# Retention and a mixture of adapters: 64-token steps instead of 128-token chunks, and queries loaded from a second queue

## The chip, the cores and the metric

One core of one Trainium2 chip runs the whole kernel. The metric is the device time of one execution in microseconds. Before the change three runs gave 181.16, 181.38 and 181.57 us, a median of 181.38.

## The reference, cut to what matters

```python
# q, k, v: (8, 8, 576, 64) float32: batch, head, token, feature
scores = scale * np.matmul(q, k.transpose(0, 1, 3, 2))
gamma = 1.0 - 2.0 ** (-5.0 - np.arange(H))
rel = pos[:, None] - pos[None, :]
Dmat = np.where(rel >= 0, gamma[:, None, None] ** rel[None], 0.0)
ret = scores * Dmat                      # causal decay instead of a softmax
x = (ret @ v)                            # then (4608, 512): heads side by side

logits = x @ w_gate                      # 8 experts
topk = the two largest logits of a token, w = their softmax
out = x + sum over both of  w * (x @ A[e]) @ B[e]     # A: 512 x 16, B: 16 x 512
```

As the decay is a power of the distance, the sum over all earlier tokens can be carried as a state: k (scaled) times v, 64 x 64 for each head. A token then needs the scores inside its own piece of the sequence and one product of its query with the state.

## The kernel before, in words

**Units.** A unit is a piece of the sequence for two of the eight batches, b = 0 and 1, with all eight heads. The sequence of 576 tokens has four chunks of 128 tokens (c = 0 to 3) and a rest of 64 (c = 4). Each full chunk gives four units, one for each pair of batches; the rest gives two units that hold four batches each, as two pieces of 64 tokens. That is NU = 18 units: 0 to 3 are chunk 0, 4 to 7 chunk 1, up to 16 and 17, the rest.

**Stages of a unit on TensorE**, by the names that the text uses, with their lines:
- T (L272): transposes k and q of a unit, heads in pairs, in halves of 64 tokens.
- S (L390) and SL (L369): scores. Each full unit has "early" tokens (the first 64) and "late" ones. S takes early keys against all 128 queries, SL late keys against late queries. VectorE multiplies S (L404, L408, L412) by a mask, or by the decay in chunk 0, and writes it next to the transposed queries, in the tile xq; SL gets its own mask (L422).
- U (L442): the unit's addition to the state, k times v over all 128 tokens. VectorE adds it to the old state (L461), and the sum is half of the next chunk's tile blk.
- X (L500; L481 in chunk 0) and XL (L523): the output. A tile blk holds, for each batch, 64 rows of state and 64 rows of early v; with the scores and the queries facing them, one product over 128 rows gives the state's part and the early part together. XL adds the late v times the late scores.
- Z (L571): logits and adapters' inner products, x times AW (136 columns).
- P (L552), B (L644), Y (L663): P transposes the weighted inner products, B transposes x back to tokens by rows, in two banks by odd and even head, and Y adds the adapters' second product into the same banks.

**The engines beside it.** ScalarE (ACT) takes most results out of PSUM: kT and xq after T (L296), xT after X (L541), zs after Z (L584), zT after P (L560), osb after Y (L680), and it copies the queries to the other 64 partitions (shift_q, L324). It also makes the sigmoid of the routing (L609). VectorE (DVE) masks, adds the state and finds the two largest logits (L594 to L599). GpSimd (POOL) scales k and q by the powers of gamma (L171), makes the routing's weights cm and zc (L619, L621), and copies v into place (place_v, L345 to L347: the early rows into blk, and one late half into vl).

**Rounds.** The body of the loop at L870 is a round t, from 3 to 17, in which unit t has its scores, unit p = t - 1 its output X and Z, unit z = t - 2 its P, B, Y, and unit t + 1 is transposed. The order of the calls is the order of the instructions on each engine. Loads of unit t + 3 and stores of unit t - 3 are all issued on SyncE's queue (SP), one after another, in a list of jobs: load_jobs, store_jobs. on_pe (L119) sums an estimate of TensorE's time, and each job is tied to the matmul at which it falls due (LOAD_NS after the last load, STORE_NS after the last store). A load of 256 KB is one of q, k, v of one batch of a unit, in runs of 64 float32. Matmuls on float32 are two records each in the trace, transposes one.

**After the rounds** the outputs of the last units are finished with their own order of calls (L906 to L948).

## Time and profile before

| | before |
|---|---|
| median of three runs | 181.38 us |
| profiled execution | 182.06 us |
| its span, first to last instruction | 180.3 us |
| granted TensorE clock, mean | 0.997 |
| busy: TensorE, weight loads, VectorE, ScalarE, GpSimd | 94%, 84%, 51%, 63%, 65% of the span |
| data moved | 39.01 MB, of which 29.11 MB are read from HBM and 9.44 MB written |
| chain that ended last | TensorE 63%, SyncE's queue 15%, DMA 9%, GpSimd 5% |

How to read it: the span lies inside the time of the execution, 1.8 us less. TensorE's row counts matmuls from start to modelled end, and they overlap, so a stage's cost is best read from the start of its first matmul to the start of the next stage's. A row of a timeline has the start and the duration of a merged run of instructions in us, engine, line, operation, what is written from what, shape (stationary rows*columns, then the moving tile) and the count; what stands in brackets is idle time of the engine before it and what ended it. In a row of windows stand the stretch, its length, the busy time of PE, PEld, DVE, ACT and POOL with the number of instructions, the granted clock, the mean share of the DMA engines' time, and GB/s. A share over 1 comes from packets that overlap on an engine.

### The profile page before, as it was taken

Reading aid. Unit: us, or ns where it says so; the run is one execution under the profiler, and the core shown is the slowest. Engines: PE = TensorE matmul, PEld = TensorE weight load, DVE = VectorE, ACT = ScalarE, POOL = GpSimd, SP = SyncE. Lnnn points to the kernel's source line nnn. Section 1 sums busy time; section 2 is a strip of 40 time slices with the busy share of each in tenths; the row PEclk is TensorE's granted clock in tenths of the full one; section 3 lists DMA queues with packets and bytes.
Section 4 is the critical chain, followed back from the end, with each engine's and each line's share of the span. In section 5 each row is a group of like instructions: output and inputs, shape, how many; then the busy total and the mean of one; then the engine's idle time right before and its main releaser. Section 6 shows DMA issues by size and latency. Waiting matters only on the chain.

```text
span 180.3 us, 9353 instructions
## 1 busy us (share of the span) xinstructions
PE 168.9 (94%) x4135; PEld 151.8 (84%) x4135; DVE 92.8 (51%) x171; ACT 114.3 (63%) x217; POOL 116.5 (65%) x176
## 2 busy tenths in 40 slices
PE   7989999989998999999999999999999999899960
PEld 2677888879887999899999999989999999899940
DVE  0082666554656383929282819190919191715540
ACT  3524296558584767676767575757777777875460
POOL 0453675699978668686969695949495958762000
PEclk9999999999999999999999999999999999999998
DMA  6999999999998998999999998989999887803306
GB/s 142 250 249 214 255 224 235 247 249 229 258 240 203 227 231 225 252 231 232 237 224 253 257 256 195 250 215 246 235 240 255 216 220 200 284 5 122 120 0 233
DMA packets 119216, 39.01 MB, mean 216 GB/s; under 512 B 114180, under 2 KB 114564, under 8 KB 119176
## 3 DMA queue, kind: packets, MB, share of 16 engines
q1 hardware_dynamic: 118304, 37.82, 84.6%
q8 instruction: 32, 0.52, 1.2%
q10 hardware_dynamic: 728, 0.47, 0.9%
q0 software_dynamic: 144, 0.13, 0.4%
q14 instruction: 8, 0.07, 0.1%
HBM read 29.11 MB, written 9.44 MB: 214 GB/s over the span
## 4 chain that ended last, share of the span: by engine, by line
PE 63%; SPq 15%; DMA 9%; POOL 5%; issue 3%; DVE 1%; ACT 1%; POOLq 0%; ACTq 0%
PE pz L571 15%; PE px L500 12%; SPq L164 11%; PE a L442 7%; DMA q<-in_q_dram 6%; PE ps_s L390 5%; PE po L644 4%; PE pt_k L272 4%; DMA v<-in_v_dram 3%; PE a L369 3%; PE pt_q L272 3%; PE po L663 3%; PE px L523 3%; SPq L160 2%; PE pzt L552 2%
## 5 line engine op out<-in xcount | busy, mean ns | idle before, releaser
L171 POOL TENSOR_TENSOR k<-k,pack 128x512 f32<-128x512 f32 x35 | 35.9, 1043 | 11.9 <-PE pt_k L272 10.4
L541 ACT COPY xT<-px 128x512 f32<-128x512 f32 x35 | 20.2, 590 | 27.5 <-PE px L500 20.4
L571 PE MATMUL pz<-AW,xT 128*128 128x136 f32 x288 | 37.6, 283 | 0.0
L571 PEld LDWEIGHTS pz<-AW,xT 128*128 128x128 f32 x288 | 34.7, 190 | 0.2
L594 DVE MAX8 m<-zs 128x8 f32<-128x8 f32 x32 | 3.8, 161 | 55.9 <-ACT zs L584 55.9
L408 DVE TENSOR_TENSOR xq<-ps_s,pack 64x1024 f32<-64x1024 f32 x24 | 29.3, 1220 | 1.7 <-PE ps_s L390 1.3
L171 POOL TENSOR_TENSOR q<-q,pack 128x512 f32<-128x512 f32 x28 | 28.8, 1042 | 1.9 <-DMA q<-in_q_dram 1.9
L500 PE MATMUL px<-xq,blk 128*64 128x128 f32 (+1 forms) x480 | 27.3, 264 | 0.1
L500 PEld LDWEIGHTS px<-xq,blk 128*64 128x64 f32 x480 | 24.2, 137 | 0.7 <-issue 0.5
L347 POOL COPY blk<-v 64x512 f32<-64x512 f32 x32 | 19.5, 608 | 1.3
L442 PE MATMUL a<-v,k 128*64 128x64 f32 x512 | 19.1, 225 | 1.0 <-issue 0.8
L390 PE MATMUL ps_s<-xq,kT 64*64 64x128 f32 (+1 forms) x640 | 19.3, 260 | 0.0
L442 PEld LDWEIGHTS a<-v,k 128*64 128x64 f32 x512 | 16.6, 138 | 2.8 <-issue 1.5
L619 POOL TENSOR_TENSOR cm<-ge,sg 128x16 f32<-128x16 f32 x16 | 3.5, 221 | 22.8 <-DVE xq L408 17.4
L680 ACT COPY osb<-po 128x512 f32<-128x512 f32 x34 | 18.0, 581 | 0.0
L461 DVE TENSOR_TENSOR blk<-a,blk 64x512 f32<-64x512 f32 x24 | 16.4, 685 | 0.2
L390 PEld LDWEIGHTS ps_s<-xq,kT 64*64 64x64 f32 x640 | 16.0, 134 | 0.5 <-issue 0.4
L296 ACT COPY xq<-pt_q 128x1024 f32<-128x1024 f32 x16 | 16.3, 1019 | 0.3 <-PE pt_q L272 0.3
L324 ACT COPY xq<-xq 64x512 f32<-64x512 f32 x26 | 16.1, 617 | 0.6
L296 ACT COPY kT<-pt_k 128x1024 f32<-128x1024 f32 x15 | 15.2, 1014 | 1.2 <-PE pt_k L272 0.6
L272 PEld LDWEIGHTS pt_k<-pack,k 64*128 64x128 f32 x288 | 10.9, 139 | 5.5 <-issue 3.7
L272 PE MATMUL pt_k<-pack,k 64*128 64x64 f32 x288 | 13.5, 230 | 1.5 <-POOL zc L621 0.8
(68 smaller groups left out, 261.2 us busy)
## 6 DMA issues: line engine op xcount, KB each, us to landing
out_dram<-osb SPq DMA_DIRECT2D x35, 256.0 KB, 4.2
q<-in_q_dram SPq DMA_DIRECT2D x28, 256.0 KB, 4.9
k<-in_k_dram SPq DMA_DIRECT2D x26, 256.0 KB, 4.9
v<-in_v_dram SPq DMA_DIRECT2D x24, 256.0 KB, 4.7
v<-in_v_dram SPq DMA_DIRECT2D x6, 512.0 KB, 6.3
k<-in_k_dram SPq DMA_DIRECT2D x5, 512.0 KB, 6.3
q<-in_q_dram SPq DMA_DIRECT2D x4, 512.0 KB, 6.4
A_nat<-in_moe_A_dram SPq DMA_DIRECT2D x1, 256.0 KB
```

Source lines behind the costliest of these rows:

```text
L164: nc.sync.dma_start(out=nt(u, w), in_=rows(w, 2 * bp, 2, 128 * c, 128))
L171: engines[b].tensor_tensor(out=tl[:, b * H : b * H + H, :], in0=tl[:, b * H : b * H + H, :], in1=g[:, c, :].unsqueeze(2).broadcast_to((128 ...
L272: nc.tensor.matmul(ps[r][:, b, hp, :], lhsT=src[hf(r), b * H + 2 * hp : b * H + 2 * hp + 2, :], rhs=id64[hf(r), :], is_transpose=True, sta ...
L296: nc.scalar.copy(out=tl.rearrange("p b a t j -> p t (b a) j"), in_=st[u]["p2" + w].rearrange("p r b a j -> p r (b a) j"),)
L347: engs[b].tensor_copy(out=blk(u)[hf(b), b], in_=vn[0:64, b * H : b * H + H, :])
L390: nc.tensor.matmul(ps[hf(b), int(ho == b), hp, qc], lhsT=kT[hf(ho), b, hp, kc], rhs=qT[hf(ho), b, hp, qc], start=(hp == 0 and qc.start == ...
L408: nc.vector.tensor_tensor(out=dst, in0=src, in1=m, op=ALU.mult)
L442: nc.tensor.matmul(a[hf(1 - b), ho, 1, hp, :], lhsT=kn[:, h, :], rhs=vn[:, h, :], start=(hp == 0), stop=True, skip_group_check=True,),
L500: nc.tensor.matmul(px[b][hf(ho), hp, qc], lhsT=bk[:, b, 2 * hp + ho, :], rhs=facing(u, b, ho)[:, hp, qc], start=(hp == 0 and t == 0 and no ...
L541: nc.scalar.copy(out=dst, in_=src)
L571: nc.tensor.matmul(st[u]["pzb"][b] if "pzb" in st[u] else pz[:, b, :], lhsT=st[u]["xT"][b][:, dt, :], rhs=AW[:, dt, :], start=(dt == 0), s ...
L680: copy(out=s["osb"][:, :, :, ho, :], in_=s["po"][ho])
```

## The change

From chunk 1 on, a unit goes by two steps of 64 tokens, as the rest did already:
- S computes the scores inside each 64-token step for both batches; SL, its mask and XL are left to chunk 0. mask_e takes one step (i) of both batches at a time.
- U gives two sums, one a step, in products over 64 tokens. add_state(t, 0) makes the state that the second step starts from, add_state(t, 1) that of the next chunk.
- A unit has two tiles, step(u, 0) and step(u, 1), each with a state half and a v half. v is loaded straight into them, in two loads of 64 partitions; place_v is left to chunk 0.
- X takes each step's 64 queries against that step's tile.
- shift_q copies the queries of a step to the other partitions, for both batches, on GpSimd.
- B transposes 128 x 128 with a whole identity (ident, a float32 copy of ident16 made by GpSimd), one bank for each batch; Y adds in three pieces of 192, 192 and 128 columns; one copy on ScalarE takes both batches out.
- A round is put in another order: X of p, U of t, S of t, P, B, Y of z, Z of p, then both transposes of t + 1. TensorE's stream has 513 instructions in such a round.
- From round 5 on, that is for units 8 to 17, q is loaded from ScalarE's queue, after evict_z; k, v and the stores stay on SyncE's, with LOAD_NS 1000 for 1150 and STORE_NS 650 for 745.
- The end has another order, and the last unit's outputs are taken out in quarters by VectorE and ScalarE.

```diff
-    LOAD_NS, STORE_NS = 1150, 745
+    LOAD_NS, STORE_NS = 1000, 650
...
+    def shift_q(u):
+        for s in range(2):
+            nc.gpsimd.tensor_copy(
+                out=of_step(st[u]["x2"][hf(1 - s)], s), in_=of_step(st[u]["qT"][hf(s)], s)
+            )
...
+        ps = st[u]["ps"] = pp.tile([128, 2, 2, HP, 64], FP32, tag="s", name="ps_s")
+        for b in range(2):
+            for hp in range(HP):
+                for s in range(2):
+                    for ho in range(2):
+                        on_pe(
+                            31,
+                            nc.tensor.matmul(
+                                ps[hf(s), int(ho == s), b, hp, :],
+                                lhsT=kT[hf(ho), b, hp, hf(s)],
+                                rhs=qT[hf(ho), b, hp, hf(s)],
...
+        a = st[u]["a"] = [
+            pp.tile([128, H, Dh], FP32, tag=f"o{s}", name=f"a{s}") for s in range(2)
+        ]
+        for h in range(H):
+            for s in range(2):
                 for b in range(2):
...
+    def add_state(u, s):
+        dst, o = next_state(u) if s else (step(u, 1), hf(0))
+        for b in range(2):
+            nc.vector.tensor_tensor(
+                out=dst[o, b], in0=st[u]["a"][s][hf(b)], in1=step(u, s)[hf(1 - s), b], op=ALU.add
+            )
...
                             nc.tensor.matmul(
-                                px[b][hf(ho), hp, qc],
-                                lhsT=bk[:, b, 2 * hp + ho, :],
-                                rhs=facing(u, b, ho)[:, hp, qc],
+                                px[b][hf(ho), hp, hf(s)],
+                                lhsT=step(u, s)[:, b, 2 * hp + ho, :],
+                                rhs=facing(u, s, ho)[:, b, hp, hf(s)],
...
+                    nc.tensor.matmul(
+                        st[u]["po"][b][:, dt, :],
+                        lhsT=st[u]["xT"][b][:, dt, :],
+                        rhs=ident,
+                        is_transpose=True,
...
+        for b in bs:
+            for ms in (slice(0, 192), slice(192, 384), slice(384, 512)):
...
     for t in range(3, NU):
...
-        jobs += lk + lq[:1] + out_jobs[:1] + lq[1:] + out_jobs[1:] + lv
+        if t < 5:
+            jobs += lk + lq[:1] + out_jobs[:1] + lq[1:] + out_jobs[1:] + lv
+        else:
+            jobs += lk + out_jobs + lv
         routing_3(z)
         routing_4(z)
-        scores(t)
-        if nxt < NU:
-            place_v(nxt, pool2)
         if t + 2 < NU:
             scale_(t + 2, "k", pool2)
             scale_(t + 2, "q", pool2)
-        if is_full(p):
+        if units[p][0] == 0:
             stage_XL(p)
+        stage_X(p)
+        evict_x(p)
         if is_full(t):
             stage_U(t)
-            add_state(t)
-        stage_X(p)
-        evict_x(p)
+        if units[t][0] == 0:
+            stage_SL(t)
+        elif is_full(t):
+            add_state(t, 0)
+        stage_S(t)
...
+        for i in range(2):
+            mask_e(t, i)
+        if units[t][0] > 0 and is_full(t):
+            add_state(t, 1)
+        if not is_full(t):
+            stage_B(z, "a", (0,))
+        stage_P(z)
+        evict_z(z)
+        for b in range(2 if 5 <= t < NU - 3 else 0):
+            load_half(t + 3, "q", b, nc.scalar)
+        stage_B(z, "a", (0, 1) if is_full(t) else (1,))
+        stage_Y(z)
+        evict_o(z)
         if nxt == NU:
             break
-        stage_T(nxt, "k")
-        evict_T(nxt, "k")
-        stage_B(z)
-        stage_T(nxt, "q")
-        stage_P(z)
-        evict_z(z)
-        evict_T(nxt, "q")
         stage_Z(p)
         routing_1(p)
-        shift_q(nxt, (nc.scalar,) * 2 if t + 2 < NU else pool2)
-        stage_Y(z)
-        evict_o(z)
+        stage_T(nxt, "k", "a")
+        evict_T(nxt, "k")
+        stage_T(nxt, "q", "s")
+        evict_T(nxt, "q")
         routing_2(p)
+        if units[nxt][0] > 0:
+            shift_q(nxt)
...
+    for b in range(2):
+        end_route_1(y, b)
+    stage_B(y, "a")
+    for b in range(2):
+        end_route_2(y, b)
+    for b in range(2):
+        stage_X(u, (b,), ("x1", "s"))
+        evict_x(u, (b,))
+    stage_P(y, tag="x0")
+    evict_z(y)
...
+    stage_Y(y)
+    evict_o(y)
+    end_bank(u, "s")
+    stage_Z(u, (1,))
...
+    stage_Y(u)
+    for b in range(2):
+        evict_end(u, b)
```

More of the change, by code (lines that the diff above doesn't have):

```diff
@@ L556, in stage_P, with evict_z @@
             )
[L558 to L561 removed]
+    def evict_z(u, bs=(0, 1)):
+        if "zT" not in st[u]:
+            st[u]["zT"] = mo.tile([128, 2, 128], FP16, tag="zT", name="zT")
+        b = slice(bs[0], bs[-1] + 1)
+        nc.scalar.copy(out=st[u]["zT"][:, b], in_=st[u]["pzt"][:, b])
     def stage_Z(u, bs=(0, 1)):
@@ L671, in stage_Y, with evict_o @@
                 )
-    def evict_o(u, vector=False):
+    def evict_o(u):
         s = st[u]
-        s["osb"] = mo.tile(
-            [128, 2, HP, 2, 64], FP32, tag="osb", name="osb", bufs=3, align_bytes=256
-        )
-        for ho in range(2):
-            copy = nc.vector.tensor_copy if vector and not ho else nc.scalar.copy
-            copy(out=s["osb"][:, :, :, ho, :], in_=s["po"][ho])
+        s["osb"] = mo.tile([128, 2, Dm], FP32, tag="osb", name="osb", bufs=3, align_bytes=256)
+        nc.scalar.copy(out=s["osb"], in_=s["po2"].rearrange("p b a m -> p b (a m)"))
     def end_route_1(u, b):
@@ L848 @@
     stage_U(2)
-    add_state(2, nc.scalar)
+    add_first(2, nc.scalar)
     stage_T(3, "k", "o")
```

346 lines of the change are left out of this document (168 added, 178 removed).

## The prediction

> **What bounds the kernel now.** I read the page first, then the busy times by window, then one round instruction by instruction, then the chain of waits.
>
> ```profile
> span 180.3 us, 9353 instructions
> ...
> PE 168.9 (94%) x4135; PEld 151.8 (84%) x4135; DVE 92.8 (51%) x171; ACT 114.3 (63%) x217; POOL 116.5 (65%) x176
> ...
> q8 instruction: 32, 0.52, 1.2%
> ```
>
> ```profile
> 70.45:79.67 9.22, 9.07 (x232) 8.45 (x231) 5.59 (x9) 6.55 (x13) 7.00 (x11) 1.00 1.06 261
> ...
> 88.72:97.72 9.00, 9.00 (x231) 8.44 (x230) 5.28 (x9) 6.54 (x13) 6.84 (x11) 1.00 0.92 229
> ```
>
> TensorE is busy in the whole of a round at full clock; DVE, ACT and POOL are at 5.3 to 7 of 9.0 us. The DMA engines stand close behind, at shares of 0.92 and 1.06. A round moves eight times 256 KB, 2.10 MB; at 229 GB/s per 0.92 that is 8.4 us of DMA time, at the 261 GB/s of the other window 8.0 us. So a round can shrink by some 0.6 us before the transfers bound it.
>
> Now TensorE in that round, by starts:
>
> ```profile
> 88.72 0.69 PE L369 MATMUL a<-xq,kT 64*64 64x64 f32 x32
> 89.24 1.05 PE L390 MATMUL ps_s<-xq,kT 64*64 64x128 f32 x32
> 90.11 0.21 PE L523 MATMUL px<-sl,vl 64*64 64x64 f32 x1
> ...
> 90.69 1.15 PE L442 MATMUL a<-v,k 128*64 128x64 f32 x32
> 91.67 1.92 PE L500 MATMUL px<-xq,blk 128*64 128x128 f32 x32
> 93.52 0.72 PE L272 MATMUL pt_k<-pack,k 64*128 64x64 f32 x16
> 94.07 0.66 PE L644 MATMUL po<-pack,xT 64*128 64x64 f32 x16
> 94.57 0.66 PE L272 MATMUL pt_q<-pack,q 64*128 64x64 f32 x16
> 95.16 0.28 PE L552 MATMUL pzt<-ident,zc 128*128 128x128 f16 x2
> 95.28 2.07 PE L571 MATMUL pz<-AW,xT 128*128 128x136 f32 x16
> 97.19 0.60 PE L663 MATMUL po<-Bcat,zT 128*128 128x256 f16 x4
> 97.72 0.69 PE L369 MATMUL a<-xq,kT 64*64 64x64 f32 x32
> ```
>
> From start to start: SL 0.52, S 0.87, XL 0.58, U 0.98, X 1.85, T of k 0.55, B 0.50, T of q 0.59, P 0.12, Z 1.91, Y 0.53; together 9.00 us and 230 matmul records.
>
> **The steps, part by part.** The shapes that the change uses instead stand at the end of the trace, where the last chunk already goes by 64 tokens:
>
> ```profile
> 153.04 1.16 PE L390 MATMUL ps_s<-xq,kT 64*64 64x64 f32 x64
> ...
> 161.27 1.16 PE L390 MATMUL ps_s<-xq,kT 64*64 64x64 f32 x64
> 162.36 2.08 PE L500 MATMUL px<-xq,blk 128*64 128x64 f32 x64
> 164.38 0.71 PE L644 MATMUL po<-pack,xT 64*128 64x64 f32 x16
> ...
> 171.50 0.71 PE L644 MATMUL po<-pack,xT 64*128 64x64 f32 x16
> ```
>
> SL and XL go (-1.10). S becomes 64 records of 64x64: 162.36 - 161.27 = 1.09. U becomes 64 records of that same tiling; S follows it without a change of tiling, which costs some 0.1 (T of q, before one, takes 0.09 more than B): 0.98, an estimate. X becomes 64 records of 64 columns: 164.38 - 162.36 = 2.02, more than now. B becomes eight whole transposes of 128 columns, which the trace does not have: Z's records take 1.91 / 16 = 0.119 us for 136 columns, so 0.112 each, 0.90; as 64 columns alone in their rows (two of T per 0.062) it would be 0.124 each, 0.99. I take 0.90, the row with the same rows and columns. Y moves the same columns in six pieces instead of four; the change of tiling behind it goes to Z: 0.47 and 2.00, estimates from 0.53 and 1.91. T twice 0.57, P 0.12. Sum: 2.02 + 0.98 + 1.09 + 0.12 + 0.90 + 0.47 + 2.00 + 1.15 = **8.73 us**, and 256 records, which with their weight loads are the 512 of the 513 instructions.
>
> The eleven rounds t = 5 to 15 last from 51.33 (quoted below) to 153.04 now, 101.7 us: eleven times 9.00 and 2.7 of stalls (below). At 8.73 without a stall they would take 96.0: **-5.7**.
>
> Other engines, in a round counted from the start of X:
>
> ```profile
> 82.62 0.22 POOL L619 TENSOR_TENSOR cm<-ge,sg 128x16 f32<-128x16 f32 x1 [1.69 <-ACT sg L609]
> 82.92 0.76 POOL L621 TENSOR_TENSOR zc<-zs,cm 128x128 f16<-128x128 f32 x2
> ...
> 84.37 0.39 SPq L160 DMA_DIRECT2D q<-in_q_dram  x1
> ...
> 86.48 0.37 ACT L560 COPY zT<-pzt 128x256 f16<-128x256 f16 x1 [0.20 <-PE pzt L552]
> ...
> 86.75 1.02 ACT L296 COPY xq<-pt_q 128x1024 f32<-128x1024 f32 x1
> ...
> 87.97 2.14 SPq L160 DMA_DIRECT2D k<-in_k_dram  x2
> ```
>
> ```profile
> L461 DVE TENSOR_TENSOR blk<-a,blk 64x512 f32<-64x512 f32 x24 | 16.4, 685 | 0.2
> ...
> L324 POOL COPY xq<-xq 64x512 f32<-64x512 f32 x2 | 1.2, 609 | 0.9 <-ACT xq L296 0.8
> ```
>
> shift_q moves from ACT to POOL, where three copies of place_v go; it now waits for ACT's eviction of q, and the routing (cm, zc) is queued behind it, and P waits for that. The eviction of k runs to 0.6, that of q to 1.6; two shifts of 0.61 to 2.9; cm and zc, 1.06 in all, to 3.9. TensorE comes to P at 2.02 + 0.98 + 1.09 = 4.1: hidden, with 0.2 to spare; what waits behind on POOL are the scalings of a unit needed two rounds later. Without that margin it would cost what zc is late.
>
> The two q loads stand on ACT between evict_z (P at 4.1 to 4.4, a copy of 0.37: done near 4.8) and evict_o, whose bank the next T of k overwrites at 7.6. Y ends near 5.8, so evict_o, 1.02 like the eviction in the row, may begin as late as 6.5. An issue takes 0.39 where its queue is free; 1.07 each where two loads go through SP, waits included. So ACT is free between 5.6 and 6.9: T waits 0 to 0.4. I take 0, since nothing else is on ACT's queue in a round, and 0.4 as the end of the range. SP keeps six issues a round instead of eight; the new spacing, 4 x 1.00 + 2 x 0.65 = 5.3 us of TensorE's time, only makes them earlier. DVE has masks of the same 1024 elements, and two state additions more (0.69 each) for a mask of 512 elements less: at most 1.4 us, in a round in which it now idles 3.7. POOL's one copy for ident falls into a wait for loads, and the buffers of blk, seven and six, come free a round before they are written. That is all hidden.
>
> **Before the rounds** the change loses. Now, at t = 3:
>
> ```profile
> 39.04 0.77 POOL L621 TENSOR_TENSOR zc<-zs,cm 128x128 f16<-128x128 f32 x2
> ```
>
> ```profile
> 39.50 0.59 PE L552 MATMUL pzt<-ident,zc 128*128 128x128 f16 x2
> ...
> 51.33 0.69 PE L369 MATMUL a<-xq,kT 64*64 64x64 f32 x32
> ```
>
> P waits for zc, which POOL makes only after the scalings of unit 4; these wait for loads, which keep their order. T and B fill that time now. In the new order P stands ahead of them and still ends near 39.9; then B 0.90, Y 0.47, Z 2.00, T 1.15: X(3) begins at 44.4. Round 4: XL 0.58, X of chunk 0 about 1.0 (S's 32 records of 128 columns take 0.87, and a change of tiling follows), U 0.98, S 1.09, a wait for zc until 48.4, then P to T, 4.64: round 5 begins at 53.0 instead of 51.33: **+1.7**.
>
> **The end.** Round 16 comes out as now (8.2: it loses the wait for a late q load, and gains one for zc). From the start of round 17 to the end of the last Z: 2.02 + 1.09 + 0.45 + 0.5 (waiting for zc) + 0.12 + 0.45 + 0.5, then Z 1.91, B 0.90, a change of tiling and X 2.1, P 0.12, Z 0.95, Y 0.5, Z 0.95 = 12.6, against 171.50 - 161.27 = 10.2 now: +2.4. Behind it:
>
> ```profile
> 174.87 2.08 SPq L948 DMA_DIRECT2D out_dram<-osb  x3
> ```
>
> SP issues its last store at the end of three, 176.95, 5.4 us after the last Z, and the span ends 3.35 later. In the new order two of them are gone by then; the route takes 1.5 and evict_z, Y and a half eviction 1.75, issue 0.65: 3.9 after Z. That is -1.4. Tail: **+1.0**.
>
> Sum: -5.7 + 1.7 + 1.0 = -3.0, and eleven times what a round stalls.
>
> **Stalls: fetching instructions.**
>
> ```profile
> 53.36 0.73 PE a L442 x18
> 54.09 0.80 issue
> ...
> 99.76 0.49 PE a L442 x10
> 100.25 0.07 issue
> ...
> 119.60 1.53 PE px L500 x26
> 121.13 0.11 issue
> ```
>
> Here TensorE stops inside a stage and waits for nothing that the profile shows. From the first to the second lie 5 x 230 - 8 matmuls, 2284 instructions with their loads; to the third 2 x 230 + 48, 1016. That is 9 and 4 times 254. The queue of instructions, q8, brings 32 packets of 0.52 MB / 32 = 16 KB; 8270 matmuls and loads by 32 is 258 a packet. So TensorE's instructions come in lines of some 256 (a few semaphore instructions a round among them), and these stops are at the borders of lines that came late. The late ones come after lines of 256 that ran in some 4.4, 5.1 and 4.2 us; most of the 32 are in time, at about 5 us a line. [...]
>
> At 513 a round the borders stay in place. The first stall is 228 instructions into round 5; 28 more precede it after the change (-12, -12, +52), so they fall some 200 and 456 into a round: past the middle of U, and in T of k. One line has Z, B and Y and lasts 5.1; the other has the end of T, X and most of U and lasts **3.6 us**. Its fetch has less time than any that I read as late. From below 0 (most are in time, and the loads are now issued early in a round); from above 5.2 - 3.6 = 1.6. I take 0.15 a round, 1.7 in all against 2.7 now, as nearer to the many in time than to the three late. Forecast: -3.0 + 1.7 = **-1.3**. The profiled execution is 182.06 with its span of 180.3; the median is 181.38, 0.4% less, so the difference is taken from that: **180.1 us**.
>
> **The rivals.**
> - Slower: the fast line stalls in every round. Place: U of each round; price 0.6 (a need of 4.2, the mean of the late ones less the early issue); it decides from 0.27 a round on. -3.0 + 6.6: 185.0. For it: 3.6 us is short; against it: most fetches pass.
> - ACT's issues take 1.07 each: ten times 0.42 besides the forecast: 184.3. For it the pair on SP; against it that SP's waits are in that row.
> - The DMA engines can't be kept above 0.92: a round of 8.4 / 0.92 = 9.1, 0.4 more than 8.73: 182.8. Against it the 1.06. [...]
> - No line stalls: -3.0, 178.4.
>
> **Chances.** Forecast 0.38, no stall 0.17, fetch 0.22, ACT 0.12, DMA 0.11. About 0.2% can be told from no change: 181.0 to 181.7. Within it lies some of the forecast's own spread (179.2 to 181.5). Faster 0.50, same 0.12, slower 0.38. The range reaches from just below the case without stalls to between the two slow ones: 178.0 to 184.6.
>
> **What would show it.** X near 2.0, U 1.0, S 1.1, B 0.9 from start to start; U begun at 53 in round 5 or later; P without a wait on zc; T of k without one on osb; ACT's loads at 0.4 to 0.8. Gaps of "issue" in every U speak for the fetch; a DMA share near 1 with POOL waiting for loads, for the transfers. A round over 9 us makes the forecast wrong.

## The result, and the profile after

| | before | after |
|---|---|---|
| median, same chip | 181.27 us (181.15 to 181.57) | 192.45 us (191.47 to 193.42) |
| ratio | | 1.063, 95% interval 1.058 to 1.068 |
| profiled execution, span | 182.06, 180.3 us | 193.34, 191.6 us |

Some executions of a kernel take over 1.5% longer than its fastest; ratios are taken without them. The change costs 6%, where 0.7% less was forecast. The page of the changed kernel (X is L557 there, U L493, S L428, P L609, B L699, Y L717, Z L629, T L287):

```profile
span 191.6 us, 9816 instructions
...
PE 170.8 (89%) x4411; PEld 154.9 (81%) x4411; DVE 98.0 (51%) x186; ACT 95.5 (50%) x178; POOL 105.1 (55%) x159
...
q1 hardware_dynamic: 97536, 32.58, 67.6%
q10 hardware_dynamic: 21528, 5.71, 13.5%
q8 instruction: 34, 0.56, 1.2%
...
PE 60%; SPq 14%; issue 7%; POOL 5%; ACT 4%; DMA 4%; ACTq 3%; DVE 1%; POOLq 0%
...
L493 PE MATMUL a<-blk,k 64*64 64x64 f32 x768 | 17.0, 223 | 8.6 <-issue 8.6
L493 PEld LDWEIGHTS a<-blk,k 64*64 64x64 f32 x768 | 14.0, 134 | 10.7 <-issue 10.0
...
L287 PEld LDWEIGHTS pt_k<-pack,k 64*128 64x128 f32 x288 | 10.8, 140 | 4.5 <-ACT osb L730 1.7
...
q<-in_q_dram ACTq DMA_DIRECT2D x20, 256.0 KB, 6.5
```

TensorE has 5 points less of the span, and most of the new idle time stands in one place: in front of U, 8.6 us that wait for nothing but "issue". q10 is ScalarE's queue, with the moved query loads, which land 6.5 us after their issue (median). Rounds, by start of X, in windows of the changed kernel (columns as in the prediction):

```profile
54.92:63.60 8.68, 8.68 (x260) 8.33 (x257) 5.26 (x7) 5.05 (x10) 6.20 (x9) 1.00 1.04 255
...
94.53:104.18 9.65, 8.96 (x261) 8.47 (x257) 5.68 (x12) 5.05 (x10) 6.20 (x9) 1.00 0.88 219
```

The first round has no stall, is filled by TensorE and lasts 8.68 us. The others have the same work and last 9.35 to 10.88. Where that goes, in the chain that ended last:

```profile
85.74 0.73 PE a L493 x38
86.47 1.92 issue
88.39 0.62 PE a L493 x25
...
96.62 0.73 PE a L493 x37
97.35 0.69 issue
98.04 0.62 PE a L493 x26
```

The stop is inside U, a little past its middle, and drifts forward by a matmul in every second round (x38 at 85.74, x37 at 96.62): a matmul is two instructions with its weight load, and 513 is one more than two lines of 256. It is the border of an instruction line (the page has 34 packets on q8 for 8822 matmuls and loads, 259 a packet). It is there in ten of the eleven rounds, 10.75 us in all from the start of the instruction before the border to the start of the one behind it (the page's 8.6 us is the idle time alone).

From start to start, the span grew by 11.3 us: up to round 5 by 54.92 - 51.33 = 3.6; rounds 5 to 15, 54.92 to 162.94, by 108.0 - 101.7 = 6.3; from there to the end by 28.7 - 27.3 = 1.4.

### The profile page after: what moved, and what is told of

Its sections match the earlier page's. It is cut to its first block, busy times and chain, and to the rows that moved or that the text cites. A ratio compares the mean times of both kernels' runs of the same rounds, so it can differ in the third digit from the quotient of the medians.

```text
span 191.6 us, 9816 instructions
## 1 busy us (share of the span) xinstructions
PE 170.8 (89%) x4411; PEld 154.9 (81%) x4411; DVE 98.0 (51%) x186; ACT 95.5 (50%) x178; POOL 105.1 (55%) x159
## 3 DMA queue, kind: packets, MB, share of 16 engines
q10 hardware_dynamic: 21528, 5.71, 13.5%
## 4 chain that ended last, share of the span: by engine, by line
PE 60%; SPq 14%; issue 7%; POOL 5%; ACT 4%; DMA 4%; ACTq 3%; DVE 1%; POOLq 0%
PE pz L629 13%; PE px L557 13%; SPq L179 9%; PE a L493 8%; PE ps_s L428 6%; PE po L699 6%; PE pt_k L287 5%; DMA k<-in_k_dram 4%; PE po L717 4%; SPq L171 3%; PE pt_q L287 3%; ACTq L171 3%; PE pzt L609 2%; ACT osb L730 2%; POOL zc L679 1%
## 5 line engine op out<-in xcount | busy, mean ns | idle before, releaser
L522 DVE TENSOR_TENSOR blk<-a,blk 64x512 f32<-64x512 f32 x48 | 33.1, 689 | 47.3 <-PE a L493 46.2
L352 POOL COPY xq<-xq 64x512 f32<-64x512 f32 x28 | 17.0, 607 | 49.1 <-ACT xq L311 44.2
L629 PE MATMUL pz<-AW,xT 128*128 128x136 f32 x288 | 38.8, 287 | 0.0
L629 PEld LDWEIGHTS pz<-AW,xT 128*128 128x128 f32 x288 | 35.6, 194 | 0.3 <-ACT xT L598 0.2
L557 PE MATMUL px<-xq,blk 128*64 128x64 f32 x896 | 29.2, 224 | 0.0
L557 PEld LDWEIGHTS px<-xq,blk 128*64 128x64 f32 x896 | 27.3, 138 | 1.0 <-issue 0.2
L730 ACT COPY osb<-po 128x1024 f32<-128x1024 f32 x17 | 17.2, 1012 | 19.5 <-PE po L717 12.4
L619 ACT COPY zT<-pzt 128x256 f16<-128x256 f16 (+1 forms) x19 | 6.9, 362 | 38.0 <-PE pzt L609 38.0
L493 PE MATMUL a<-blk,k 64*64 64x64 f32 x768 | 17.0, 223 | 8.6 <-issue 8.6
L493 PEld LDWEIGHTS a<-blk,k 64*64 64x64 f32 x768 | 14.0, 134 | 10.7 <-issue 10.0
L699 PE MATMUL po<-ident,xT 128*128 128x128 f32 x144 | 19.8, 279 | 0.0
L428 PE MATMUL ps_s<-xq,kT 64*64 64x64 f32 x896 | 16.5, 219 | 0.0
L699 PEld LDWEIGHTS po<-ident,xT 128*128 128x128 f32 x144 | 15.9, 143 | 0.2
L428 PEld LDWEIGHTS ps_s<-xq,kT 64*64 64x64 f32 x896 | 15.2, 135 | 0.1
L287 PEld LDWEIGHTS pt_k<-pack,k 64*128 64x128 f32 x288 | 10.8, 140 | 4.5 <-ACT osb L730 1.7
L287 PE MATMUL pt_k<-pack,k 64*128 64x64 f32 x288 | 13.4, 232 | 1.1 <-ACT osb L730 1.1
```

What stands on the lines that cost most here:

```text
L287: nc.tensor.matmul(ps[r][:, b, hp, :], lhsT=src[hf(r), b * H + 2 * hp : b * H + 2 * hp + 2, :], rhs=id64[hf(r), :], is_transpose=True, sta ...
L428: nc.tensor.matmul(ps[hf(s), int(ho == s), b, hp, :], lhsT=kT[hf(ho), b, hp, hf(s)], rhs=qT[hf(ho), b, hp, hf(s)], start=(b == 0 and hp == 0),
L493: nc.tensor.matmul(a[s][hf(b), h, :], lhsT=kn[hf(s), b * H + h, :], rhs=step(u, s)[hf(s), b, h, :], start=(h == 0), stop=True, skip_group_ ...
L522: nc.vector.tensor_tensor(out=dst[o, b], in0=st[u]["a"][s][hf(b)], in1=step(u, s)[hf(1 - s), b], op=ALU.add)
L557: nc.tensor.matmul(px[b][hf(ho), hp, hf(s)], lhsT=step(u, s)[:, b, 2 * hp + ho, :], rhs=facing(u, s, ho)[:, b, hp, hf(s)], start=(hp == 0 ...
L629: nc.tensor.matmul(st[u]["pzb"][b] if "pzb" in st[u] else pz[:, b, :], lhsT=st[u]["xT"][b][:, dt, :], rhs=AW[:, dt, :], start=(dt == 0), s ...
```

## The experiments

The kernels ran in groups, each group on one chip; between the chips the median of the kernel before differs by up to 2% (181.03 to 185.04 us). So each has its ratio to the kernel before on its own chip. All edits are to the changed kernel unless told otherwise.

**The changed kernel again**, as a reference on the chip of three kernels below, q_early, q_sync_shift28 and q_sync_prol (as_changed).

> The changed kernel itself, to have its time and its stalls on the chip on which the next three run: 1.06 times the kernel before, stalls in U of 0.9 to 1.1 us a round from the sixth unit on, lines entered at T of k with 2 to 3 us from the entry to the start of the next fetch.

Ratio 1.050 (1.039 to 1.062). Stalls in U were 5.4 us in all from start to start, half of what was expected, and waits of T of k for the eviction of the outputs rose (the rows count idle time alone):

```profile
L493 PE MATMUL a<-blk,k 64*64 64x64 f32 x768 | 16.3, 223 | 3.8 <-issue 3.6
...
L287 PEld LDWEIGHTS pt_k<-pack,k 64*128 64x128 f32 x288 | 10.8, 140 | 6.9 <-ACT osb L730 4.2
```

So what a round loses differs between executions of one kernel. The waits of T of k have a cause of their own: in two rounds the second query load of ScalarE was issued 2.6 us after the end of the first issue, because it waited for a semaphore that it shares with a transfer of SyncE (a store issued at 57.37 landed at 61.62, the load was issued at 61.64), and the eviction stood behind it.

**Phase** (shift28, shift144). First theory: a line needs a fixed 4.5 us from its entry to the next, so only the length of the line before a border counts.

```diff
-    fill(8)
+    fill(8, cuts=(3, 3, 3, 3, 3, 3, 3))      # 28 instructions more
+    fill(8, cuts=(10, 10, 10, 10, 10, 10, 10, 10))   # or 144 more
```

> 28 more instructions on TensorE before the rounds (the filling matmuls at the start are cut into three parts each, with the same columns in all), nothing else. Theory (fetch): TensorE's instructions come in lines of 256, a line needs some 4.5 us from its entry until the next one is usable, and rounds of 513 hold the two borders where the line before is 3.55 us (T, X and 80 instructions of U) and the other 5.15. With 28 more, the borders lie 50 instructions into U and 13 before T: both lines hold some 4.35 us of work, and the stalls in U fall from 10.8 us in all to 2 to 4. Time 184 to 187. Rival (the loads from ScalarE's queue, or the denser loads, hold the round up): nothing changes, 192 within 1.

> 144 more instructions on TensorE before the rounds, by cutting the filling matmuls into ten. Theory (fetch): the borders lie 62 instructions into X and 63 into S; the line between them (half of X, U, half of S) holds 1.05 + 0.98 + 0.53 = 2.56 us of work against some 4.5 for the fetch, so the stall leaves U and stands in the middle of S with 1.9 us a round, about twice what it was: 11 x (1.9 - 1.0) = +10, time 199 to 206. Rival (a wait for loads or a DMA queue): the stall stays in U, time 192 within 1.5.

28 more: ratio 1.078 (1.060 to 1.096); 144 more: 1.061 (1.039 to 1.084). The rows of the two pages:

```profile
L636 PE MATMUL pz<-AW,xT 128*128 128x136 f32 x288 | 40.6, 290 | 4.3 <-issue 4.3
...
L500 PE MATMUL a<-blk,k 64*64 64x64 f32 x768 | 16.0, 223 | 4.2 <-issue 4.1
```

```profile
L435 PE MATMUL ps_s<-xq,kT 64*64 64x64 f32 x896 | 19.1, 221 | 7.3 <-issue 7.0
```

The stalls went where the borders went: into Z (L636) and U (L500) with 28 more, into the middle of S (L435) with 144. So they belong to line borders, not to U or its data. But the sizes refute the fixed 4.5: lines with 4.35 us of work stalled at both borders (4.3 us idle in Z, 4.2 in U, over all rounds), and the line with 2.56 us stalled for only 0.3 to 0.7 in six of the eleven rounds. The time of a fetch depends on something else. The records of the trace say on what. For each line: when TensorE enters it, when the next 16-KB packet of q8 begins after that, and when the line behind it starts:

```
144 more,  line entered   packet starts   packet   next line     q1    q10
in X           77.66        +2.05           0.92     +4.53       1.05   0.07
in X          116.12        +0.28           1.33     +2.90       0.39   0.05
changed kernel
in T of k      72.37        +2.06           0.92     +4.45       0.86   0.29
in T of k      93.56        +1.88           1.03     +4.48       0.51   0.23
in T of k     151.43        +2.80           1.21     +5.36       0.57   0.38
```

(q1 and q10: share of the 16 engines' time that packets of SyncE's and ScalarE's queue took from the entry to the end of the fetch.) In this profile of the changed kernel no fetch of the rounds begins before the line ahead of it is entered. (In as_changed two began 0.4 us earlier, one of them while TensorE waited at T of k.) The packet takes 0.9 to 1.3 us in these rows, the line can be used about 1.4 later (4.45 - 2.06 - 0.92 = 1.47); what varies is the start, from 0.28 at shares of 0.39 and 0.05 to 2.80 at 0.57 and 0.38. Behind T of k stands 3.55 us of work, so a start up to 3.55 - 1.05 - 1.4 = 1.1 after the entry is hidden, and what is later is seen. Second theory, then: the fetch waits for the transfers, and ScalarE's loads are in flight when the line at T of k asks.

**The loads of ScalarE's queue**, put back on SyncE's (q_sync):

```diff
-        if t < 5:
-            jobs += lk + lq[:1] + out_jobs[:1] + lq[1:] + out_jobs[1:] + lv
-        else:
-            jobs += lk + out_jobs + lv
+        jobs += lk + lq[:1] + out_jobs[:1] + lq[1:] + out_jobs[1:] + lv
...
-        for b in range(2 if 5 <= t < NU - 3 else 0):
-            load_half(t + 3, "q", b, nc.scalar)
```

> All query loads from SyncE's queue again, with the pacing of the changed kernel; the 64-token steps and the rounds of 513 stay. Theory (fetch): the stalls in U stay at about 1.0 a round; only the late evictions of the outputs on ScalarE (1.3 us before T of k) go: 190 to 192. Rival (ScalarE's issues or its queue's transfers cause the stalls): U runs through and the time falls to 184 or less.

Ratio 1.023 (1.006 to 1.039), beside 1.061 to 1.080 of the three others on that chip:

```profile
q1 hardware_dynamic: 118336, 37.82, 81.1%
...
L493 PE MATMUL a<-blk,k 64*64 64x64 f32 x768 | 15.8, 222 | 2.0 <-issue 1.7
```

The same bytes, all on q1, and 1.7 us of stalls before U. By its ratio the time is 185.4 us where the kernel before takes 181.3: between what the two theories expected, nearer to the rival.

The same loads on ScalarE's queue, but issued earlier (q_early):

```diff
+        for b in range(2 if 5 <= t < NU - 3 else 0):
+            load_half(t + 3, "q", b, nc.scalar)
         stage_X(p)
         evict_x(p)
...
         evict_z(z)
-        for b in range(2 if 5 <= t < NU - 3 else 0):
-            load_half(t + 3, "q", b, nc.scalar)
```

> The ten units' query loads stay on ScalarE's queue, but are issued ahead of the evictions of X instead of after the eviction of the routed factors: some 3 us earlier in a round. Theory (traffic: the fetch that U needs is asked at T of k, 7.5 us into a round, and waits there behind the transfers of ScalarE's queue, which last some 6.5 us from the issue): the transfers are over by 8.3 to 9 us of the round instead of 11.4, so the start of the fetch comes 0.9 to 1.6 us after the entry instead of 2.0 to 3.0 and the stalls in U fall to 0.2 to 0.5 a round; the late outputs (1.3 us) go too; the evictions of X come 0.8 to 1.5 us later, of which B may wait for up to 1. Time 3 to 8 us under the changed kernel. Theory (phase alone: line of 3.55 us against a fetch of 4.5): U keeps 0.9 to 1.1 a round, time within 1.5 us of the changed kernel. Rival (a second queue is slower whatever its place): the same.

Ratio 1.055 (1.044 to 1.066), no gain beside 1.050. The stall moved:

```profile
L493 PE MATMUL a<-blk,k 64*64 64x64 f32 x768 | 16.4, 223 | 3.3 <-issue 3.0
...
L287 PE MATMUL pt_k<-pack,k 64*128 64x64 f32 x288 | 15.0, 233 | 4.5 <-issue 4.5
```

U stalls less, as expected; T of k, which never stalled at its border in the changed kernel, has 4.5 us now. That second half was not expected. The starts of the fetches explain it, means of the lines 11 to 29:

```
                asked at T of k: start     q1    q10 | asked in U: start     q1    q10
changed         2.19 (1.50 to 3.00)       0.55  0.36 | 1.55 (1.06 to 2.39)  0.79  0
q_early         1.35 (1.04 to 2.06)       0.60  0.01 | 3.32 (2.61 to 4.26)  0.72  0.43
q_sync          1.39 (0.48 to 2.11)       0.90  0    | 1.90 (1.41 to 3.05)  0.85  0
before          1.55 (0.44 to 3.25)       0.92  0    | 1.72 (0.46 to 2.92)  0.96  0
```

(In the kernel before the borders drift, so its two columns are odd and even lines.) With loads early in a round, the fetch asked in U meets q10's transfers, and waits twice as long (3.32 us against 1.55 in the changed kernel); there the line lasts 5.1 us, and still is too short. The other fetch is free of q10 and starts as with one queue. The wait follows the transfers of the second queue from one border to the other. How long it is at T of k differs much between executions: the means are 1.60, 2.02 and 2.44 us in the other three profiles with ScalarE's loads at the old place (as_changed, and route and pace below), and 0.92, 1.69, 1.75 and 1.92 in the other four with one queue and the same line (q_sync_prol, q_sync_prol_2, q_sync_route, q_sync_route_pace below). The groups overlap, so 2.19 against 1.39 alone would show little; the 3.32 of q_early lies outside of both.

Then without that traffic (q_none). The kernel leaves out the query loads of the last ten units, which read the queries of units 6 and 7:

```diff
-        return tiles(u // 2, w)[:, u % 2]
+        return tiles(3 if w == "q" and u >= 8 else u // 2, w)[:, u % 2]
...
-        for b in range(2 if 5 <= t < NU - 3 else 0):
-            load_half(t + 3, "q", b, nc.scalar)
```

> The changed kernel without the query loads of the last ten units: their steps read the queries of the units two before, so 5.2 MB of 39 are not moved, ScalarE issues nothing in the rounds and its queue carries nothing there; SyncE's loads and stores, their pacing, every engine's arithmetic and the phase of the lines stay. Theory (the traffic of ScalarE's queue delays the fetch): the next fetch starts 0.3 to 1.5 us after T of k, stalls in U of 0 to 0.3 a round, 2 us in all or less, no late outputs, time 178 to 183. Rival (SyncE's loads alone, or the dense line whatever the traffic, make most of the stall): stalls in U of 0.6 or more a round, time 187 or more.

Ratio 0.997 (0.992 to 1.001), median 182.38. Its profiled execution, of 185.60 us, by windows and in the chain:

```profile
56.54:66.61 10.07, 8.86 (x259) 8.38 (x256) 5.46 (x9) 5.04 (x10) 6.81 (x10) 1.00 0.94 232
...
84.28:95.06 10.78, 8.96 (x260) 8.48 (x257) 5.74 (x12) 5.06 (x10) 6.20 (x9) 1.00 0.83 210
95.06:103.72 8.66, 8.66 (x259) 8.32 (x256) 5.62 (x11) 5.03 (x10) 6.20 (x9) 1.00 0.72 188
```

```profile
59.36 1.21 issue
87.10 1.81 issue
```

In the first four rounds the engines are still full (0.83 to 0.99), and U stalls by 1.2 and 1.8 us, which makes more than the 2 expected; the median is 3.2 us lower, so a typical execution may not have them. From 95 us on seven rounds last 8.66 to 8.68 each without any stall, with the same instructions at the same borders as in the changed kernel: the share is 0.72 or less, and a fetch starts 0.11 to 0.54 us after T of k is entered (1.04 in the first of them). From the entry to the end of these fetches the share is only 0.16 to 0.36: they meet a pause of the transfers. For those asked in U it is 0.98 to 1.13, and they start 1.1 to 2.0 us after the entry, which the longer line hides. So the short line alone, at the phase of 513 instructions, does not stall; it takes transfers at the moment of the fetch.

One part of the change in the kernel before (before_q_act):

```diff
-        jobs += lk + lq[:1] + out_jobs[:1] + lq[1:] + out_jobs[1:] + lv
+        jobs += lk + out_jobs + lv          # from t = 5 on
...
         shift_q(nxt, (nc.scalar,) * 2 if t + 2 < NU else pool2)
+        for b in range(2 if 5 <= t < NU - 3 else 0):
+            load_half(t + 3, "q", b, nc.scalar)
```

> The kernel before with one part of the change: the query loads of the same ten units issued from ScalarE's queue (after the two shifts of the queries, ahead of the eviction of the outputs); its 128-token steps, its order and its pacing of 1150 and 745 stay. Theory (a fetch asked while ScalarE's queue transfers waits for it): entries to fetch starts go from 0.5 to 3.2 us to 2 to 4 where the queue is busy, the stalls at line borders go from 2.1 us in all to 5 to 8, time 3 to 6 us over the kernel before. Rival (the second queue hurts only because the new order has a dense stretch behind its fetch): stalls of 2 to 3 us, time within 1 of the kernel before.

Ratio 1.020 (1.013 to 1.026), some 3.5 us. The time is as the first theory expected, the way is not. Two rows of its page, in U (L442) and at T of k (L272):

```profile
L442 PE MATMUL a<-v,k 128*64 128x64 f32 x512 | 19.4, 225 | 0.9 <-issue 0.8
...
L272 PEld LDWEIGHTS pt_k<-pack,k 64*128 64x128 f32 x288 | 11.0, 140 | 4.8 <-issue 3.2
```

The same rows in the kernel before are no shorter:

```profile
L442 PE MATMUL a<-v,k 128*64 128x64 f32 x512 | 19.1, 225 | 1.0 <-issue 0.8
...
L272 PEld LDWEIGHTS pt_k<-pack,k 64*128 64x128 f32 x288 | 10.9, 139 | 5.5 <-issue 3.7
```

From start to start the stalls at line borders in rounds 5 to 15 are 3.7 us against 2.0 in the kernel before, where 5 to 8 were expected, and the fetches start 2.03 and 2.23 us after the entry on average, against 1.55 and 1.72. A part of the rest is no fetch: one round lasts 10.64 us, since B waits there for the eviction of the outputs behind two issues of ScalarE,

```profile
73.18 3.25 ACTq L160 DMA_DIRECT2D q<-in_q_dram  x2
```

of 0.41 and 0.45 us, with 2.4 between them, in which the second waits for a semaphore that it shares with a load of SyncE (issued at 71.39, landed at 75.96). So moving the loads alone costs a third of what the whole change costs, by both ways, and that the time lay in the expected range is in part luck. Whether the longer lines of that order are why the fetches cost less there was not tested.

**Pacing** put back (pace; LOAD_NS, STORE_NS = 1150, 745):

> Only the pacing of loads and stores put back to 1150 and 745. Theory (fetch): the phase and the line lengths are the same, so 191 to 193, with the stalls in U between 0.8 and 1.1 a round. Rival (denser transfers make the fetch late): the stalls in U fall to half or less, 187 or less.

Ratio 1.080 (1.066 to 1.093): not better, so the denser issuing is not what makes the stalls. They are longer than expected, 0.6 to 3.1 a round; as the changed kernel itself ran on other chips, that is not put down to the pacing.

**The prologue.** P of the second unit waits 2.5 us, and behind it TensorE runs slower, in the changed kernel:

```profile
36.15:39.69 3.54, 1.02 (x45) 0.78 (x34) 3.31 (x7) 0.00 (x0) 3.46 (x6) 1.00 1.08 244
39.69:46.71 7.02, 6.89 (x93) 6.46 (x97) 1.90 (x6) 2.62 (x4) 4.34 (x5) 0.76 1.10 248
```

```profile
39.69 0.59 PE L609 MATMUL pzt<-ident,zc 128*128 128x128 f16 x2 [2.52 <-POOL zc L679]
40.11 1.56 PE L699 MATMUL po<-ident,xT 128*128 128x128 f32 x8
41.47 1.06 PE L717 MATMUL po<-Bcat,zT 128*128 128x192 f16 x6
42.32 2.85 PE L629 MATMUL pz<-AW,xT 128*128 128x136 f32 x16
...
51.33 0.60 PE L717 MATMUL po<-Bcat,zT 128*128 128x192 f16 x6
51.77 2.07 PE L629 MATMUL pz<-AW,xT 128*128 128x136 f32 x16
```

The granted clock is 0.76 over the stretch; Y and Z take 1.06 and 2.85 us, a round later 0.60 and 2.07. Two ways to fill the wait: the routing ahead of four scalings on GpSimd (route), or, with the loads on SyncE's queue, B and Z ahead of P (q_sync_prol):

```diff
-    for w in "kq":
-        scale_(4, w, pool2)                 # ahead of the loop
...
         routing_4(z)
+        if t == 3:
+            for w in "kq":
+                scale_(4, w, pool2)
```

```diff
+        if t == 3:
+            stage_B(z, "a")
+            stage_Z(p)
         stage_P(z)
         evict_z(z)
```

> The changed kernel with one edit in its prologue: the scaling of the fifth unit's keys and queries on GpSimd is issued after the routing factors of the second unit, not ahead of them. Theory (P of the second unit waits 2.8 us for four scalings of 1.04 each that GpSimd does first, and TensorE's clock is halved behind that wait): P comes at 37, no slice of the granted clock drops, round 5 begins 2.5 to 3.5 us earlier, and the time falls by 2 to 3.5; the stalls in U stay. Rival (the transposes of the fifth unit then wait for the late scaling): round 5 begins less than 1 us earlier.

> Query loads all from SyncE's queue; in the round of the fourth unit alone B and Z of the units before go ahead of P, so that TensorE has 2.9 us of work where it waited for the routed factors. Theory (the wait at P and the halved clock after it cost 1.6 us beside the wait of 2.8): round 5 begins 2.5 to 4.5 us earlier than with the query loads from SyncE alone (some 54.4), the granted clock stays at 1 there, time 2.5 to 4 us lower. Rival (the chain of routing or the loads hold the rounds of the fourth and fifth unit up whatever TensorE does): the wait moves on to the next P or T, round 5 begins at 53.5 or later, and the time falls by less than 1.

The first: ratio 1.058 (1.049 to 1.067), no gain, though round 5 begins at 52.55 instead of 54.92. By windows, and ScalarE behind it:

```profile
30.00:42.16 12.16, 12.16 (x291) 11.13 (x292) 6.69 (x15) 6.97 (x14) 8.29 (x12) 1.00 1.01 228
...
52.55:65.89 13.34, 9.68 (x260) 9.08 (x257) 6.35 (x12) 5.29 (x10) 6.81 (x10) 0.89 1.04 246
```

```profile
58.10 4.72 ACTq L171 DMA_DIRECT2D q<-in_q_dram  x2
62.92 1.01 ACT L730 COPY osb<-po 128x1024 f32<-128x1024 f32 x1 [5.03 <-DMA blk<-in_v_dram]
```

The prologue runs through at full clock, and round 5 then takes 13.3 us: two issues of ScalarE stand there from 58.10 to 62.83, the eviction of the outputs behind them, and T of k waits 3.3 us for it; the granted clock falls to 0.89. The issues themselves take 0.40 and 0.39 us. The 3.9 between them are a wait for a semaphore that the second shares with a store of SyncE, issued at 56.59 and landed at 62.42. So what was won was lost to a second queue that waited for the first.

The second: ratio 1.004 (0.999 to 1.009), round 5 at 53.40 against 54.42 in q_sync, a gain of 1.0 there where 2.5 to 4.5 was expected; the clock stays at 1, but T of k then waits 1.1 for the next eviction. Its later rounds show something that the removed loads could not:

```profile
98.97:107.65 8.68, 8.68 (x260) 8.33 (x256) 5.64 (x11) 5.05 (x10) 6.21 (x9) 1.00 1.03 253
```

Five rounds, from 98.97 to 142.38, last 8.68 or 8.69 each without a stall, with all loads, at shares of 0.95 to 1.03. The fetches asked at T of k start 0.44 to 0.74 us after the entry there. So neither the amount of traffic nor a share near 1 is enough for a stall. What in the transfers ahead of the fetch makes the difference, the runs do not settle.

The two together, and with the old pacing (q_sync_route, q_sync_route_pace):

> The two edits together: all query loads from SyncE's queue, and the scaling of the fifth unit after the routing factors. If both theories hold: rounds of 8.7 to 9.0 us with some 2 to 4 us of stalls in all, round 5 from 51.5 to 52, time 178.5 to 181 where the kernel before has 181, ratio 0.985 to 1.0. If the traffic theory is wrong: 1.02 or more.

> The same with the pacing of the kernel before (1150 and 745). Eight jobs then fill 8.4 us of a round of 8.7 instead of 7.3, so SyncE's queue has fewer gaps, but shorter ones in which loads stand in line. Theory (a fetch waits for what is in line ahead of it): the same within 1 us, stalls spread over more rounds. Rival (the loads come too late at the slower pace, or the fetch gets free stretches): over 1 us slower, or over 1 us faster.

Ratio 1.018 (1.010 to 1.026); with the old pacing six executions took 184.59 to 190.83 us, the first of these some 1.01. Slower than expected, and near the 1.02 that stood for a wrong traffic theory: round 5 begins at 54.24, since U of round 4 stalls and the granted clock falls to 0.86 there, and the pages have 5.7 and 8.1 us of issue in front of U with one queue alone:

```profile
42.10:54.24 12.14, 9.66 (x257) 8.90 (x249) 5.69 (x10) 4.68 (x10) 10.01 (x13) 0.86 0.96 234
```

**The short line with one queue.** Three ways to lengthen it: 28 instructions more (q_sync_shift28); B between X and U (q_sync_prol_b, with q_sync_prol_2 as its reference); and that with P ahead of S (q_sync_prol_b2).

> Query loads all from SyncE's queue, and 28 more instructions before the rounds, so that both lines hold some 4.35 us of work. Theory (traffic and phase together): with one queue the next line is usable 3.6 to 4.5 us after an entry, so 4.35 covers most of it: stalls of 0 to 0.2 us a round at the borders (in U and in Z), 1 us in all or less, and a time 2 to 3.5 us under that of all query loads from SyncE at the old phase, level with the kernel before within 1.5 us. Theory (the fetch has a fixed place among the loads, phase does not matter): stalls of 3 to 4 us in all, as at the old phase.

> Query loads from SyncE's queue and the prologue's order with B and Z ahead of P once more, on the chip of the two beside it: a ratio of 0.995 to 1.015, stalls at borders of 2 to 5 us in all.

> The same with B of every round between X and U instead of behind P: 16 instructions of 0.88 us go from the slow line into the fast one, the lines hold 4.3 and 4.35 us at the old phase, and the rounds stay at 513. Theory (a line stalls by what its work falls short of the fetch, which takes 3.5 to 4.6 us with one queue): stalls of 1 to 3 us in all, and a time 0 to 3 us under the kernel beside it. Rival (both borders now stand at the edge, as with 28 instructions more): 4 to 6 us of stalls, level or up to 2 us slower.

```diff
         evict_x(p)
+        if t > 3 and is_full(t):
+            stage_B(z, "a")
         if is_full(t):
             stage_U(t)
```

28 more: 1.015 (1.002 to 1.029), with stalls of 0.1 to 1.6 in most rounds, 6.0 in all, of which 5.3 in Z: more than either theory expected. The reference: 1.012 (1.000 to 1.025); its profiled execution, of 195.32 us, has 5.8 us of issue in front of U. B ahead of U: 1.2 us of issue there, but a ratio of 1.030 (1.023 to 1.037):

```profile
98.55 0.28 PE L609 MATMUL pzt<-ident,zc 128*128 128x128 f16 x2
99.30 0.61 PE L717 MATMUL po<-Bcat,zT 128*128 128x192 f16 x6 [0.47 <-ACT zT L619]
```

B was what covered the eviction of P's result; without it Y waits, 0.68 us from P's second record to Y in every round. I had not seen that. The last kernel puts P ahead of S, so that S covers it, and the routing ahead of the shifts on GpSimd:

```diff
+        early = t > 4 and is_full(t)
+        if early:
+            stage_P(z)
+            evict_z(z)
         stage_S(t)
...
         routing_4(z)
+        if units[t][0] > 0:
+            shift_q(t)
```

> Query loads from SyncE's queue, the prologue's order with B and Z ahead of P, B between X and U in every round, and now P ahead of S, so that S covers the eviction of the routed factors and Y waits for nothing; for P to have its factors there, GpSimd does the routing ahead of the two shifts of the queries. Theory (the short line is the remaining cause with one queue, and the 0.68 before Y was B's missing cover): no wait before Y, 1 to 3 us of stalls at borders in all, rounds of 8.7 to 9.0 us, time 3 to 7 us under the kernel with B ahead of U alone, a ratio of 0.985 to 1.01 to the kernel before. Rival (a round of 8.7 us leaves the 2.1 MB of its transfers no room, and TensorE then waits for loads or for P): rounds of 9.2 or more, with the time in waits for POOL, a ratio of 1.015 or more.

Ratio 1.020 (1.013 to 1.026), slower than expected, with no wait before Y and fewer stalls at borders, 3.2 us in all. A stretch of 9 us:

```profile
101.00:110.00 9.00, 9.00 (x262) 8.33 (x260) 5.69 (x10) 5.00 (x10) 6.24 (x9) 1.00 0.98 247
```

Six of the eleven rounds last 9.05 us, without a stall; the other five lose 0.1 to 1.3. The order itself is thus 0.37 longer than 8.68; that this comes of B and P (full rows) now standing between stages of half rows was not tested. So a longer line hides the fetch in more of the rounds, and in this order its price is as large as the gain. Of all these kernels with the whole computation none was faster than the kernel before.

## Why the prediction was wrong

**Rounds without stalls: right.** 8.73 was forecast, 8.68 measured, with each stage within 0.05.

**What hides beside TensorE: right for GpSimd and VectorE, too small for ScalarE.** P had its factors in the rounds. T of k was given 0 with a bound of 0.4; in three rounds it waited, 1.3 us in all, behind an issue of ScalarE that took up to 2.2 us, not the 1.07 of the bound:

```profile
78.69 0.39 ACTq L171
79.12 2.20 ACTq L171
81.44 1.02 ACT osb L730
```

In this round, the longest of the three waits, a shorter issue would not have helped: a store whose landing the eviction waits for too came at 81.30, and the issue ended at 81.32. What the prediction did not price is that ScalarE's second load can wait for a transfer of SyncE to land, as in as_changed and route (up to 3.9 us).

**Stalls: the step that failed.** "I take 0.15 a round, 1.7 in all" was 10.75. The place was right: past the middle of U, in the line of 3.6 us, and none in T of k. So was the rival, at 0.6 a round; it measured 1.0. The wrong part is the reason for the small value, "the loads are now issued early in a round". That was thought of SyncE's loads. The trace of the kernel before could have told more: its fetches start 1.55 and 1.72 us after the entry on average, and with 1.05 for the packet and 1.4 behind it the next line is usable after 4.0 to 4.2 us (an estimate from these rows), later than a line of 3.6 lasts. The many that were in time had lines of about 5 us, as the prediction says itself, and were counted as if they spoke for this one. That a line's fetch has only the time of the line ahead of it, as the price takes it, was the author's assumption, which no row of the prediction shows; in the trace of the changed kernel each fetch of rounds 5 to 15 does start after that line is entered, by 0.1 to 3.0 us. And the two loads moved to ScalarE go out about 5 us into a round:

```profile
99.97 1.01 ACTq L171 DMA_DIRECT2D q<-in_q_dram  x2
```

That is 5.4 into the round from 94.53; they land 6.5 later (median), and the fetch that U needs is asked in between, at T of k, 7.5 into a round without a stall. They were priced as time of ScalarE and as a share of the engines, never as something ahead of a fetch. q_none shows that without them the same lines pass (from its fifth round on), q_early that the wait goes where they go. But it is not the second queue alone: with the same loads on one queue and the same line, the pages of executions of 181.31, 189.33, 187.48, 195.32 and 189.54 us have 1.4, 1.7, 5.7, 5.8 and 8.1 us of issue in front of U, and q_sync_prol, the first of them, ran five rounds with all of the traffic and no stall. So the stall is a late fetch, one that starts up to 3.00 us (changed kernel, T of k) or 4.26 us (q_early, U) after the entry, against 0.11 to 0.54 in the pauses of q_none; how the two queues share in it, and what sets the spread, was not settled.

**Before the rounds: +1.7 forecast, +3.6 measured.** P began at 39.69, near where forecast. Not seen was that the wait of 2.5 us would cost the clock: it was granted at half from 40.48 on for 3.4 us, and B, Y and Z took 1.35, 0.85 and 2.78 from start to start instead of 0.88, 0.44 and 2.00, 1.7 us; in route, where P did not wait there, it stayed at 1.00 up to 42.16. **The end: +1.0 forecast, +1.4 measured.** (The forecast's own figures, 3.9 for 5.4 us, make -1.5 and not -1.4 behind the last Z.)

**The transfers as a bound:** the first round ran at a share of 1.04, and five rounds of q_sync_prol at 0.95 to 1.03 in 8.68 us, so 0.92 is no limit of the engines, as that rival had it.

## What to carry to other kernels

Find the borders of TensorE's instruction lines first (here every 256 instructions: at 513 a round the stop moved by one matmul in every second round), and ask for each what is being transferred when the line ahead of it is entered: that traffic can be part of the fetch's time, on ScalarE's queue (the fetch asked in U started after 3.32 us with q10 at a share of 0.43 in q_early, after 1.55 with q10 at 0 in the changed kernel) as on SyncE's alone (in q_none after 1.1 to 2.0 us at shares of 0.98 to 1.13, after 0.11 to 0.54 at 0.16 to 0.36). The mean share of the engines does not tell it: the fetches of T of k started after 0.44 to 0.74 us in rounds of q_sync_prol at 0.95 to 1.03, and after 2.3 us in the changed kernel's first round, at 1.04. Rounds of 513 instructions put the same border on the same stage each time: the short line stalled in ten of eleven rounds of the changed kernel, and, without the query loads, in none of the last seven of q_none. And a load moved to another engine's queue has to be priced three times: as time of the engine that issues it (an issue of ScalarE took up to 2.20 us in the changed kernel, and in route the second stood 3.9 us waiting for a transfer of SyncE's queue), as share of the transfers (13.5% of the span on q10), and as traffic at the moment when a fetch is asked.

## What the runs showed of the hardware beside that

- A fetch of 16 KB took 0.9 to 1.3 us in most cases, up to 2.22 in the changed kernel, and was usable some 1.4 later; its start lay between 0.1 us (q1 at a share of 0.16) and 4.3 us (q_early, asked in U) after the line ahead of it was entered, but for the two of as_changed that began 0.4 us before it.
- The granted clock fell to half for 3.41 us, or twice that, behind single waits of TensorE from 1.88 us (as_changed, before P) to 3.71 us (pace, before P), but stayed at 1.00 behind others of 2.92 us (shift144, before P) and 2.91 us (pace, in U). So the length of a wait alone does not decide it.
- One DMA issue of ScalarE took from 0.37 to 2.20 us in the rounds of the changed kernel. Between two of them lay 0.04 us, or up to 3.9 (route) where the second waited for a semaphore that it shares with a transfer of SyncE; in each case of more than 1 us the semaphore's last step came 0.02 or 0.03 us before the issue.
